# Splitting a fold on GpSimd over two slots, and re-timing what stands around it, in a fused Fourier-mixing and gated-MLP kernel

## The chip, the core and the metric

The kernel runs on one core of a Trainium2 chip, as one launch. The metric is the device time of that launch in microseconds (us), as a median over runs. Five engines work side by side and meet through semaphores: TensorE (PE in the profile; its weight loads are listed apart as PEld), VectorE (DVE), ScalarE (ACT), GpSimd (POOL) and SyncE (SP, which here only issues transfers). Each engine takes its own instructions in program order.

## The reference

The input x has 8 batches of 3008 rows of 256 values. Each batch goes through a two-dimensional Fourier transform of which the real part is kept, and every one of the 24064 rows then goes through a two-layer block with a sigmoid gate, 256 to 2048 to 256:

```python
X = np.fft.fft(x, axis=1)
X = np.fft.fft(X, axis=2)
x = X.real.astype(np.float32).reshape(24064, 256)
h = x @ w_in
g = h * (1.0 / (1.0 + np.exp(-1.702 * h)))
out = g @ w_out
```

All inputs and outputs are float32, and w_in and w_out arrive as float64 words that the kernel converts itself.

## The kernel before, in words

The transform along the rows is split as 3008 = 47 x 64 and done in two levels of small matrix products; the transform along the 256 columns is folded into w_in once (`fold_w`), so that the block works on half as many columns with real and imaginary parts (`wcs`). The output product uses a fast scheme of block matrix multiplication (seven products for eight), one level inside each step and a second level over pairs of steps: the sums and differences it needs come from `sums` and `deeper` on the activations and from `differences` and `small_weights` on w_out.

**Steps and slots.** The work is a list of 384 steps: 8 batches (b), 3 blocks each (blk), 2 halves (hh), and 8 pairs of hidden blocks (p, NP = 8). A batch is therefore 48 steps, and `t0 = 48 b` is its first. The main loop runs over slots t; a slot holds parts of several steps:

- `begin(t + 1)` and `second(t)`: the two halves of the hidden product x, each 8 matmuls of 128x64 weights (`L478`, tile x). Step t uses the PSUM bank `b0` or `b1` by the parity of t.
- `product(t - 3, 0)`, `product(t - 3, 1)`, and `small_products`: the output products into banks `o0` to `o4` (tile po, `L478` and `L623`).
- `middle`, `forward`, `activate_back` on ACT (`L542`, `L555`, `L562`).
- On DVE, in this order: `backward(t)` (`L503`, reads x from PSUM), `doubled(t + 1)` (`L548`, reads x from PSUM and has to be done before `second(t + 1)` may add to the same bank), `sums(t - 2)` (`L577`, `L578`), `deeper` (`L595`, twice a slot), and once in eight slots the steps that combine and store an output tile (`L703`, `L726`, `L745`, `L677`).
- On POOL: `sums(t - 1)` (`L574`, `L575`), two of the four sums of a step.

The first 8 steps are different: they use `hidden`, `rows` and `activate`, need one PSUM bank more each, and run while w_in and w_out are still being converted.

**The next batch.** Beside the block for batch b, the transform of batch b + 1 is prepared. `extra` holds calls by slot; they run at the end of their slot, in the order in which they were put down. `turn` and `load_x` bring x in; `fold1(b, c, nc.gpsimd)`, for c = 0 to 7, adds mirrored rows and columns of x in place on POOL (`L201`, `L203`, `L205`, `L206`, for c = 0 also `L195` to `L197`); `mix1(b, m)`, for m = 0 to 3, multiplies two folded chunks by the first-level matrices on PE (`L230`, tile ps) and copies the result back to xt on ACT (`L233`); `spill`, `fill` and `rotate` turn the layout through DRAM; `stage2` is the second level (`L332`, with the transposes `L338` on DVE).

**PSUM banks.** There are eight: b0 to b2 and o0 to o4. `bank(name)` without a tag takes the next of the list `spare`. For the first slots the list is b0, b1, b2, o4; from slot 8 on it is set at the end of every slot t to b2 and `b{t % 2}`, so that `mix1` and `stage2` in slot t take the bank in which the x of step t was, and begin(t + 2) needs it next:

```python
        if t >= NP:
            spare[:] = ["b2", f"b{t % 2}"]
```

In slot t with (t - 3) divisible by 8, from slot 11 on, a new output tile begins and `begin(t + 1)` is put ahead of `product(t - 3, 0)`.

Of the kernel before, what the change touches and what calls it, by code (L numbers as in the profile page):

```python
# [29 lines left out]
ALU = mybir.AluOpType  # L30
# [9 lines left out]
NU, NG = 2, 12  # L40
# [10 lines left out]
def free(ap, offset, *dims):  # L51
    return bass.AP(ap.tensor, ap.offset + offset, [list(ap.ap[0])] + [list(d) for d in dims])
# [59 lines left out]
def kernel(ctx: ExitStack, tc, x, w_in, w_out, tab1, tab2, out):  # L112
    nc = tc.nc
    B, S, D = x.shape
    DF = w_in.shape[1]
    H = D // 2
# [10 lines left out]
    op = ctx.enter_context(tc.tile_pool(name="op", bufs=2, space=SB))  # L127
# [21 lines left out]

        return w[rows, jj * NM:jj * NM + 64]  # L150

    spare = ["b0", "b1", "b2", "o4"]

    def bank(name, tag=None):
        if tag is None:
            tag = spare.pop(0)
            spare.append(tag)
        return psp.tile([128, 512], F32, tag=tag, name=name)
# [25 lines left out]

    e0 = {}

    def fold1(b, c, eng):

        t = xt[0:64 + NA]
        if c == 0:  # L190

            e, t0 = cv.tile([NA, 2, D], F32, tag="e", name="e"), xt[0:NA]
            e0[b] = e
            fwd, rev = free(t0, 1, [31 * D, 2], [1, H - 1]), free(t0, D - 1, [31 * D, 2], [-1, H - 1])
            eng.tensor_tensor(e[:, :, 1:H], fwd, rev, op=ALU.add)  # L195
            eng.tensor_copy(free(e[:], 0, [D, 2], [H, 2]), free(t0, 0, [31 * D, 2], [H, 2]))
            eng.tensor_tensor(e[:, :, H + 1:D], fwd, rev, op=ALU.subtract)  # L197

        at, up = 2 * c * D, (31 - 2 * c) * D
        ends = free(t, up, [-D, 2], [H, 2])  # L200
        eng.tensor_tensor(ends, ends, free(t, at, [D, 2], [H, 2]), op=ALU.add)  # L201
        low = free(t, at + 1, [D, 2], [1, D - 1])
        eng.tensor_tensor(low, low, free(t, up + D - 1, [-D, 2], [-1, D - 1]), op=ALU.add)  # L203
        fwd, rev = free(t, at + 1, [D, 2], [1, H - 1]), free(t, at + D - 1, [D, 2], [-1, H - 1])
        eng.tensor_tensor(free(t, up + 1, [-D, 2], [1, H - 1]), fwd, rev, op=ALU.add)  # L205
        eng.tensor_tensor(free(t, up + H + 1, [-D, 2], [1, H - 1]), fwd, rev, op=ALU.subtract)  # L206
# [114 lines left out]
    def stage2(b, blk):  # L321

        pq, t4 = pqp.tile([128, 2, 512], F32, tag="pq", name="pq"), t4t[b]
        pqt[b, blk] = pq
        m = m2 if b else m2f
        ps = [bank("ps2") for _ in range(NU)]
        for cs in range(2):
            for h in range(2):
                for g in range(4):
                    for u in range(NU):  # L330
                        rows, at = slice(64 * u, 64 * u + 64), cs * 256 + h * 128
                        nc.tensor.matmul(ps[u][32 * g:32 * g + 32, at:at + 128], lhsT=m[rows, cs, h * RUN:(h + 1) * RUN],  # L332
                                         rhs=t4[rows, 4 * blk:4 * blk + 4, cs * H + 32 * g:cs * H + 32 * g + 32],
                                         start=True, stop=True)
        for cs in range(2):
            for u in range(NU):

                nc.vector.transpose(free(pq[:], cs * 512 + u * RUN, [256, 2], [NU * RUN, 4], [1, RUN]),  # L338
                                    free(ps[u][:], cs * 256, [128, 2], [32, 4], [1, 32]))
# [46 lines left out]
    def low_up(key, lo=0, n=1024):  # L386

        nc.scalar.activation(pre[key][2][:, lo:lo + n].bitcast(F32), raw[key][:, lo:lo + n, 0], ACTF.Copy, scale=2.0 ** -29,
                             bias=2.0 ** 23)
# [72 lines left out]
    NP = NF // 2  # L462
# [5 lines left out]
    def width(t):  # L468

        return 226 if steps[t][1:3] == (0, 1) else 256  # L470

    def two(ap, n):
        return free(ap, 0, [256, 2], [1, n])

    def halves(out, lhs, rhs, **how):

        for c0 in (0, 64):
            nc.tensor.matmul(out[c0:c0 + 64], lhsT=lhs[:, c0:c0 + 64], rhs=rhs, skip_group_check=True, **how)  # L478

    def operands(t, cs, i):  # L480
        b, blk, hh, p = steps[t]
        f = 2 * p + i
        return wcs[cs][:, f * 128:(f + 1) * 128], pqt[b, blk][:, cs, hh * 256:hh * 256 + width(t)]

    def hidden(t):

        n = width(t)
        pa, pb = bank("pa"), bank("pb")
        for ps, cs in ((pa, 0), (pb, 1)):
            for i in range(2):  # L490
                halves(ps[:, i * 256:i * 256 + n], *operands(t, cs, i), start=True, stop=True)
        v = sp.tile([128, 512], F32, tag="v", name="v")
        nc.scalar.copy(two(v[:], n), two(pa[:], n))
        vb[t] = v, pa, pb
# [28 lines left out]
    def begin(t):  # L523

        n = width(t)
        x = xb[t] = bank("x", f"b{t % 2}")
        for i in range(2):
            halves(x[:, i * 256:i * 256 + n], *operands(t, 0, i), start=(i == 0), stop=False)
# [28 lines left out]
    def backward(t):  # L557
        reversed_sum(t, gt.pop(t), xb.pop(t), ALU.subtract)
# [237 lines left out]
    ends = n0 + 4 - 28 * NM  # L796
# [72 lines left out]
    def at(t, fn, *args):  # L869
        extra.setdefault(t, []).append((fn, args))  # L870
# [16 lines left out]
    at(4, rotate, 0, 4, NG)  # L887
    for i in range(NCK):
        at(7 + i, differences, i)
        at(9 + i, small_weights, i)  # L890
    for b in range(B):
        t0 = b * NBLK * NF
        late = 0 if b else 3
        if b + 2 < B:
            at(t0 + 10, turn, b + 2)
        if b + 1 < B:
            for c in range(NCH):
                at(t0 + 7 + 2 * c + late, fold1, b + 1, c, nc.gpsimd)
                if c % 2:
                    at(t0 + 8 + 2 * c + late, mix1, b + 1, c // 2)  # L900
            at(t0 + 24 + late, spill, b + 1)
            at(t0 + 29 + late, fill, b + 1)
            if b + 2 < B:
                at(t0 + 33 + late, load_x, b + 2)
            at(t0 + 36 + late, rotate, b + 1)
        for blk in range(NBLK):
            nxt = (b, blk + 1) if blk + 1 < NBLK else (b + 1, 0)
            if nxt[0] < B:
                at(t0 + blk * NF + 8, stage2, *nxt)
                at(t0 + blk * NF + 9, nyquist, *nxt)  # L910

    for t in range(n + LAG):
        if t < NP:
            hidden(t)
            if t == 0:
                low_up(in2)
                nyquist(0, 0)
                low_down(in2)
            if t in rows_at:
                first_row(rows_at[t])  # L920
            if t >= LAG:
                for part in range(2):
                    product(t - LAG, part)
            if t in early:
                fold_w(early[t])
            if t:
                activate(t - 1)
            rows(t)
            if t == NP - 1:
                for ahead in range(2):  # L930
                    middle(NP + ahead)
                begin(NP)
        else:
            if t < n:
                if t + 2 < n:
                    middle(t + 2)
                second(t)
            heads = [(product, t - LAG, 0)] + [(begin, t + 1)] * (t + 1 < n)
            for fn, *args in heads[::-1] if t >= NP + LAG and (t - LAG) % NP == 0 else heads:
                fn(*args)  # L940
            product(t - LAG, 1)
            small_products(t - LAG, (1, 2, 4, 7))
            small_products(t - LAG - 1, (5, 6, 3))
            if t == NP:
                activate(t - 1)
            if t < n:
                forward(t)
            if NP < t <= n:
                activate_back(t - 1)
                sums(t - 1, nc.gpsimd)  # L950
            swap(t - LAG - 2)
            if t < n:
                backward(t)
        if NP <= t + 1 < n:
            doubled(t + 1)
        if t >= NP:
            sums(t - 2, nc.vector)
            deeper(t - 2, 0)
            deeper(t - 3, 1)
        if t >= LAG:  # L960
            combine(t - LAG)
            combine_small(t - LAG - 1)
            combine_last(t - LAG - 2, 0)
            combine_last(t - LAG - 3, 1)
        if t == NP:
            held += [hp.tile(shape, F32, tag="h", name="held") for shape in
                     ([128, 2, 4, 2, 64], [128, 2, 4, 2, 64], [128, 4, 256], [128, 1024])]
        if t >= NP:
            spare[:] = ["b2", f"b{t % 2}"]
        for fn, args in extra.get(t, ()):  # L970
            fn(*args)

# [27 lines left out]
```

## Time and profile before

| What | Value |
|---|---|
| Median of 3 runs | 1928.61 us (1924.86 to 1929.21) |
| Span of the profiled execution | 1926.1 us, granted TensorE clock 0.996 |
| PE busy | 1892.3 us, 98% of the span |
| DVE busy | 1549.2 us, 80% |
| ACT busy | 875.6 us, 45% |
| POOL busy | 786.5 us, 41% |
| Transfers | 104.92 MB, mean 54 GB/s |

The first line is what is compared. The profile is of one execution with each instruction's start and end. Busy time on PE is a union of overlapping matmuls, so a wait on PE shows as idle time only where it is longer than the tail of the matmul before it; shares of the whole span are means over stages that differ. The stretch of a batch in which the next batch is folded and mixed is slots t0 + 7 to t0 + 22; in the last batch there is nothing to fold, so that the same slots there show the block alone.

### The profile page before, as it was taken

Reading aid. Unit: us, or ns where it says so; the run is one execution under the profiler, and the core shown is the slowest. Engines: PE = TensorE matmul, PEld = TensorE weight load, DVE = VectorE, ACT = ScalarE, POOL = GpSimd, SP = SyncE. Lnnn points to the kernel's source line nnn. Section 1 sums busy time; section 2 is a strip of 40 time slices with the busy share of each in tenths; the row PEclk is TensorE's granted clock in tenths of the full one; section 3 lists DMA queues with packets and bytes.
Section 4 is the critical chain, followed back from the end, with each engine's and each line's share of the span. In section 5 each row is a group of like instructions: output and inputs, shape, how many; then the busy total and the mean of one; then the engine's idle time right before and its main releaser. Section 6 shows DMA issues by size and latency. Waiting matters only on the chain.

```text
span 1926.1 us, 51018 instructions
## 1 busy us (share of the span) xinstructions
PE 1892.3 (98%) x21392; PEld 1376.7 (71%) x21392; DVE 1549.2 (80%) x3011; ACT 875.6 (45%) x1868; POOL 786.5 (41%) x1073
## 2 busy tenths in 40 slices
PE   8989999999999999999999999999999999999998
PEld 5666877767776777767777677776777767778775
DVE  7658787888788877898778977888787988878876
ACT  5634444444444444444444444444444444444442
POOL 4475223643245432463235532355223652223332
PEclk9999999999999999999999999999999999999999
DMA  8731360336212362214523164032631232202201
GB/s 279 164 50 14 81 87 18 51 49 115 24 14 49 49 120 18 35 28 72 98 18 50 22 109 56 15 58 44 101 33 23 18 48 47 29 13 18 24 16 23
DMA packets 145398, 104.92 MB, mean 54 GB/s; under 512 B 104914, under 2 KB 127986, under 8 KB 143984
## 3 DMA queue, kind: packets, MB, share of 16 engines
q1 hardware_dynamic: 143952, 101.14, 31.4%
q8 instruction: 167, 2.74, 0.6%
q10 hardware_dynamic: 1216, 0.52, 0.1%
q14 instruction: 63, 0.52, 0.1%
HBM read 58.38 MB, written 48.01 MB: 55 GB/s over the span
## 4 chain that ended last, share of the span: by engine, by line
PE 83%; DVE 11%; ACT 3%; POOL 1%; issue 1%; DMA 0%; SPq 0%; DVEq 0%; ACTq 0%; POOLq 0%
PE po L478 37%; PE x L478 29%; PE po L623 12%; DVE r L595 4%; DVE h L503 2%; DVE g L548 1%; PE ps L332 1%; PE ps L230 1%; DVE s L577 1%; DVE s L578 1%; ACT xt L233 1%; DVE held L577 1%; PE ps L283 1%; ACT g L542 1%; DVE os L677 1%
## 5 line engine op out<-in xcount | busy, mean ns | idle before, releaser
L478 PE MATMUL x<-pq,wcs 128*64 128x256 f32 (+1 forms) x6016 | 771.5, 377 | 9.0 <-DVE g L548 4.6
L555 ACT ACTIVATE h<-x 128x512 f32<-128x512 f32 (+1 forms) x376 | 221.5, 589 | 793.1 <-PE x L478 697.3
L478 PE MATMUL po<-s,wo 128*64 128x256 f32 (+1 forms) x4512 | 571.6, 375 | 3.0 <-DVE s L577 1.9
L478 PEld LDWEIGHTS x<-pq,wcs 128*64 128x64 f32 x6016 | 426.7, 137 | 180.8 <-issue 12.3
L574 POOL TENSOR_TENSOR s<-h 128x256 f32<-128x256 f32 (+1 forms) x282 | 204.6, 726 | 852.4 <-issue 614.6
L478 PEld LDWEIGHTS po<-s,wo 128*64 128x64 f32 x4512 | 334.0, 137 | 150.6 <-DVE s L577 2.3
L503 DVE TENSOR_TENSOR h<-g,x 128x512 f32<-128x512 f32 (+2 forms) x440 | 255.5, 592 | 208.7 <-ACT h L555 208.1
L542 ACT ACTIVATE g<-nb,af 128x256 f32<-128x256 f32 (+1 forms) x752 | 335.4, 496 | 2.0 <-DVE h L512 0.8
L548 DVE SCALAR_TENSOR_TENSOR g<-x,g 128x512 f32<-128x512 f32 (+1 forms) x376 | 254.4, 677 | 76.5 <-PE x L478 76.2
L478 PE MATMUL po<-h,wo 128*64 128x256 f32 (+1 forms) x1824 | 264.9, 376 | 0.7 <-DVE u L703 0.7
L562 ACT ACTIVATE h<-h 128x512 f32<-128x512 f32 (+1 forms) x376 | 231.1, 615 | 0.2 <-DVE h L503 0.2
L575 POOL TENSOR_TENSOR s<-h 128x256 f32<-128x256 f32 (+1 forms) x282 | 208.6, 740 | 0.0
L595 DVE TENSOR_TENSOR r<-h 128x256 f32<-128x256 f32 (+1 forms) x368 | 205.1, 598 | 0.0
L478 PE MATMUL po<-held,wo 128*64 128x256 f32 (+1 forms) x1504 | 194.1, 375 | 0.0
L623 PE MATMUL po<-r,held 128*64 128x128 f32 (+1 forms) x2208 | 185.6, 271 | 0.0
L478 PEld LDWEIGHTS po<-h,wo 128*64 128x64 f32 x1824 | 136.5, 137 | 59.9 <-DVE u L703 1.2
L577 DVE TENSOR_TENSOR s<-s,h 128x256 f32<-128x256 f32 (+1 forms) x282 | 167.0, 592 | 3.3 <-POOL s L574 3.3
L623 PEld LDWEIGHTS po<-r,held 128*64 128x64 f32 x2208 | 143.2, 137 | 23.2
L574 POOL TENSOR_TENSOR held<-h 128x256 f32<-128x256 f32 (+1 forms) x94 | 69.0, 734 | 212.0 <-DVE held L726 94.0
L478 PEld LDWEIGHTS po<-held,wo 128*64 128x64 f32 x1504 | 111.7, 137 | 49.3 <-DVE held L577 1.6
L578 DVE TENSOR_TENSOR s<-h,s 128x256 f32<-128x256 f32 (+1 forms) x282 | 133.3, 473 | 9.7
L623 PE MATMUL po<-h,wo 128*64 128x128 f32 (+1 forms) x1472 | 112.3, 270 | 0.0
(106 smaller groups left out, 1717.3 us busy)
## 6 DMA issues: line engine op xcount, KB each, us to landing
out_dram<-os SPq DMA_DIRECT2D x284, 64.0 KB
Td<-xt SPq DMA_DIRECT2D x14, 768.0 KB
t<-Td SPq DMA_DIRECT2D x7, 1536.0 KB
xt<-in_x_dram SPq DMA_DIRECT2D x14, 512.0 KB
xt<-Xr SPq DMA_DIRECT2D x14, 512.0 KB
nb<-pq SPq DMA_DIRECT2D x23, 256.0 KB
out_dram<-os SPq DMA_DIRECT2D x96, 56.0 KB
Xr<-in_x_dram SPq DMA_DIRECT2D x7, 752.0 KB
```

Source lines behind the costliest of these rows:

```text
L478: nc.tensor.matmul(out[c0:c0 + 64], lhsT=lhs[:, c0:c0 + 64], rhs=rhs, skip_group_check=True, **how)
L503: nc.vector.tensor_tensor(free(h[:], 512 + at + m - 1, [256, 2], [RUN, blocks], [-1, m]), *ins, op=op)
L542: nc.scalar.activation(g[:, i * 256:i * 256 + n], nbt[b, blk][:, hh * 256:hh * 256 + n], ACTF.Copy, scale=af2[:, f:f + 1])
L548: nc.vector.scalar_tensor_tensor(g, two(xb[t][:], n), 2.0, g, op0=ALU.mult, op1=ALU.add)
L555: nc.scalar.activation(two(h[:], n), two(xb[t][:], n), ACTF.Gelu_apprx_sigmoid)
L562: nc.scalar.activation(g, g, ACTF.Gelu_apprx_sigmoid)
L574: eng.tensor_tensor(s1, a21, a22, op=ALU.add)
L575: eng.tensor_tensor(s3, a11, a21, op=ALU.subtract)
L577: eng.tensor_tensor(s2, s1, a11, op=ALU.subtract)
L578: eng.tensor_tensor(s4, a12, s2, op=ALU.subtract)
L595: nc.vector.tensor_tensor(out, i0, i1, op=how)
L623: nc.tensor.matmul(sub(k)[64 * side:64 * side + 64, :w], lhsT=lhs, rhs=rhs, start=(p == 0 and k in (1, 2)), stop=(p == NP - 2), skip_group ...
```

## The change

It has six parts, all of them about when things are done; the arithmetic stays as it is.

1. `fold1` is cut in two parts: part 0 (`L201`, `L203`, and for c = 0 also the three operations on e) and part 1 (`L205`, `L206`). Part 0 goes in the slot where the whole fold went, part 1 in the next slot.
2. `mix1` therefore moves one slot back, to t0 + 11, 15, 19 and 23. For the first batch `late` grows from 3 to 4 on top: parts of folds in slots 11 to 26, mixes in 15, 19, 23 and 27. `rotate` stays where it was.
3. `small_weights` moves ahead: from slots 9 to 12 to slots 8, 8, 9, 10.
4. `spare` has six banks in the first slots (o2 and o3 are added); in slots 6 and 7 it is cut to the o banks and b2, so that b0 and b1 are free.
5. `begin(8)` moves, in slot 7, from the end of the slot to a place ahead of the output products of step 4.
6. From slot 8 on `spare` is `b{t % 2}`, b2 in place of b2, `b{t % 2}`; and `stage2` does the transposes of one bank first, then those of the other.

Part 1 of the fold is meant to spread POOL's work evenly over the slots, parts 3 to 5 to shorten the start, part 6 to free the bank that x needs next sooner.

```diff
-    spare = ["b0", "b1", "b2", "o4"]
+    spare = ["b0", "b1", "b2", "o2", "o3", "o4"]
...
-    def fold1(b, c, eng):
+    def fold1(b, c, part, eng):
...
-        eng.tensor_tensor(ends, ends, free(t, at, [D, 2], [H, 2]), op=ALU.add)
-        low = free(t, at + 1, [D, 2], [1, D - 1])
-        eng.tensor_tensor(low, low, free(t, up + D - 1, [-D, 2], [-1, D - 1]), op=ALU.add)
+        if part == 0:
+            eng.tensor_tensor(ends, ends, free(t, at, [D, 2], [H, 2]), op=ALU.add)
+            low = free(t, at + 1, [D, 2], [1, D - 1])
+            eng.tensor_tensor(low, low, free(t, up + D - 1, [-D, 2], [-1, D - 1]), op=ALU.add)
+            return
...
-        for cs in range(2):
-            for u in range(NU):
+        for u in range(NU):
+            for cs in range(2):
...
-        at(9 + i, small_weights, i)
+        at(max(7 + i, 8), small_weights, i)
...
-        late = 0 if b else 3
+        late = 0 if b else 4
...
-                at(t0 + 7 + 2 * c + late, fold1, b + 1, c, nc.gpsimd)
+                for part in range(2):
+                    at(t0 + 7 + 2 * c + part + late, fold1, b + 1, c, part, nc.gpsimd)
                 if c % 2:
-                    at(t0 + 8 + 2 * c + late, mix1, b + 1, c // 2)
+                    at(t0 + 9 + 2 * c + late, mix1, b + 1, c // 2)
...
-            at(t0 + 36 + late, rotate, b + 1)
+            at(t0 + 36 + 3 * (late > 0), rotate, b + 1)
...
+            if t == NP - 2:
+                spare[:] = [tag for tag in spare if tag[0] == "o"] + ["b2"]
             hidden(t)
+            if t == NP - 1:
+                begin(NP)
...
-                begin(NP)
...
-            spare[:] = ["b2", f"b{t % 2}"]
+            spare[:] = [f"b{t % 2}", "b2"]
```

More of the change, by code (lines that the diff above doesn't have):

```diff
@@ L185 @@
     e0 = {}
-    def fold1(b, c, eng):
+    def fold1(b, c, part, eng):
         t = xt[0:64 + NA]
-        if c == 0:
+        if c == 0 and part == 0:
             e, t0 = cv.tile([NA, 2, D], F32, tag="e", name="e"), xt[0:NA]
```

## The prediction, made before the change was run

> **What bounds the kernel now.** I read the page's first part, then the busy time by stretches, then the order of time around the places where PE stops.
>
> ```profile
> PE 1892.3 (98%) x21392; PEld 1376.7 (71%) x21392; DVE 1549.2 (80%) x3011; ACT 875.6 (45%) x1868; POOL 786.5 (41%) x1073
> ```
>
> PE sets the end, and only 33.8 us of its span are idle. The first stretch below is slots t0+11 to t0+26 of a batch with six of its eight folds in it, the second the same slots of the last batch, which folds nothing (columns: length, then busy time of PE, PEld, DVE, ACT, POOL).
>
> ```profile
> 813.57:894.20 80.63, 78.81 (x937) 56.46 (x938) 69.02 (x127) 37.31 (x84) 41.77 (x57) 1.00 0.31 56
> 1741.18:1813.21 72.03, 72.03 (x866) 60.67 (x864) 57.84 (x127) 33.42 (x76) 22.10 (x33) 1.00 0.19 19
> ```
>
> PE has four mixes more in the first: 1.46 + 3 x 1.02 = 4.5 us by the chain of waits. The rest, 80.63 - 72.03 - 4.5 = 4.1 us, is lost. Idle time shows only 1.8 of it, because each wait also costs the overlap of matmuls: one lasts 376 ns and a new one starts every 108 ns (20 in 2.16 us), so an interruption costs some 0.27 us beside the idle time. With the same number of instructions DVE is busy 11.2 us longer. Its L595 alone (the same stretches, DVE only):
>
> ```profile
> 813.57:894.20 80.63, 21.63 (x32) 1.00 0.31 56
> 1741.18:1813.21 72.03, 12.13 (x32) 1.00 0.19 19
> ```
>
> The order of time shows why:
>
> ```profile
> 827.76 1.27 POOL L203 TENSOR_TENSOR xt<-xt 111x510 f32<-111x510 f32 x1
> 827.88 1.40 DVE L577 TENSOR_TENSOR held<-held,h 128x226 f32<-128x226 f32 x1
> ...
> 829.11 0.75 POOL L205 TENSOR_TENSOR xt<-xt 111x254 f32<-111x254 f32 x1
> ...
> 829.32 0.80 DVE L578 TENSOR_TENSOR held<-h,held 128x226 f32<-128x226 f32 x1
> ...
> 829.83 0.88 POOL L206 TENSOR_TENSOR xt<-xt 111x254 f32<-111x254 f32 x1
> 830.04 2.47 DVE L595 TENSOR_TENSOR r<-h 128x226 f32<-128x226 f32 x2
> ...
> 833.06 0.64 DVE L503 TENSOR_TENSOR h<-g,x 128x448 f32<-128x448 f32 x2
> 833.63 0.61 DVE L548 SCALAR_TENSOR_TENSOR g<-x,g 128x452 f32<-128x452 f32 x1
> ...
> 833.85 1.08 PE L230 MATMUL ps<-xt,w 47*64 47x256 f32 x12 [0.59 <-DVE h L503]
> ```
>
> While POOL folds, L577 takes 1.40 us, not 0.38, and the two L595 2.47, not 0.8: one whole fold in one slot makes DVE 3.1 us late here. L503 then comes late, and the mix on PE waits for the bank it reads. In the first batch POOL itself is late:
>
> ```profile
> 118.95 0.60 PE L478 MATMUL po<-s,wo 128*64 128x226 f32 x4 [1.91 <-DVE s L577]
> 127.47 0.70 PE L230 MATMUL ps<-xt,w 47*64 47x256 f32 x3 [4.63 <-POOL xt L206]
> ```
>
> **What the skill says.** The Trainium skill, "SBUF — State Buffer", section "SBUF: two separate sides", says that a DVE operation with two SBUF inputs and a GpSimd operation that reads SBUF take turns on a shared port pair, the loser blocked for the whole instruction of the other. The trace agrees: L577 ends 0.25 us after the L203 beside it. L503 and L548, with one input in PSUM, keep their 0.65 and 0.61 us under folds. "PSUM — Partial Sum Buffer", section "PSUM bank collisions raise a hardware error", wants accesses of different engines to a bank kept apart by semaphores per bank, not per address; so a mix has to wait for L503, and the next x for the copy L233.
>
> **Part by part: splitting the folds (1) and moving the mixes (2), batches 1 to 6.** Nothing is added; eight folds of 0.36 + 1.33 + 0.77 + 0.80 = 3.3 us become halves of 1.7 and 1.6. A slot is 4.65 us of PE (37.2 for eight). DVE needs 0.69 + 0.69 + 0.42 + 0.43 + 2 x 0.40 = 3.0 us of it, plus 2.0, 1.6, 1.4 and 0.7 in the four combining slots t0+10 to 13 (and 18 to 21). A fold makes DVE 11.2 / 6 = 1.9 us longer on average: 1.0 where it met combining steps that read PSUM (slot 11), 3.1 where it didn't (13). Now a plain slot takes 3.0 + 1.1 = 4.1 us with half a fold, which fits; before, every odd slot had up to 3.0 + 3.1 = 6.1.
>
> What PE lost by slot (start of second(t) to the next, against the same slot without folds): slot 11 0.45 and slot 19 0.4, x waiting for the mix's second copy on ACT; the mix after slot 14 1.2; slot 16 0.8, x waiting for L548 (0.63 idle); six more at 0.1 to 0.17: 3.7 us.
>
> - The ACT waits (0.85) go: the mixes leave the slots ahead of 11 and 19, where begin() stands first, and the bank that x needs is now copied first (part 6): free 0.6 us sooner, and behind one more product of 0.43 us. L233 ended 0.29 us too late.
> - The 1.2 at the mix and the 0.8 at slot 16 go if DVE is at most 1.5 us behind its usual start in slots 15 and 16, 1.75 us after second(). By the sums above it is behind 1.6 us in slot 11 (from 10: 5.0 + 1.1 against 4.45), and then the half fold falls beside L703, L503 and L548, which it doesn't block; 0.4 in slot 12, 0.7 in 13, 0.6 in 14, about none from 15. L548 may end as late as 4.2 us into a slot of that width; in slot 11 the mix behind it leaves 5.7.
> - I keep 1.1 us per batch for what combining and half folds still cost in slots 10 to 13 and 18 to 21, and for the mix now waiting with its first matmul for the bank, not its fifth. Gain 2.6 x 6 = 15.6 us; ends 0.85 x 6 = 5 and 3.7 x 6 = 22.
>
> **The first batch (2, 3).** second(13) to second(15) took 134.35 - 115.70 = 18.65 us; two slots of 4.2 and a mix of 1.46 make 9.9: 8.8 lost to POOL being late. POOL works without pause from 91.1 us: four differences at 0.79, small weights at 1.8 for four, sums at 1.3, the first fold 4.9. New order: sums(10) end at 114.9 (118.65 before), while product(10) needs them near 116.5; the folds of chunks 0 and 1 end near 127, and the mix, now after slot 15, is due at about 128. I take 8.3 of the 8.8. The four later waits (at 155.29, 156.54, 169.03 and 187.61: 0.72, 0.16, 0.52, 0.32, and 4 x 0.27) are 2.8 us, of the kind above: 1.7 of them. Together 10.0; ends 5 and 11.6.
>
> **The start (4, 5).** x of step 8 waited 0.80 us for L548, which waited for begin(8) behind 3.5 us of products; now begin(8) stands ahead of them, DVE comes to L548 at 90.6, not 91.1, and 0.5 to 1.0 us goes. pb waited 1.38 us for a bank at 45.72, pa 0.34 at 62.06, pb 0.24 at 85.44: six banks take these away, but ACT and DVE, preparing weights, are busy 30 and 32 of 50 us there, so that PE may wait for them instead. I take 2.0 in all; ends 0.5 and 4.
>
> **The rest (6).** The four transposes of stage2 free the first bank 0.7 us sooner; only slot 24 of the first batch (0.32 at 187.61) waited for that, counted above. The later spill has five slots or more to fill(); no engine waits for it in the list of waits, and rotate() comes 6 slots (28 us) after fill in the first batch, 7 before: nothing.
>
> Sum: 15.6 + 10.0 + 2.0 = 27.6; 1928.6 - 27.6 = **1901.0 us**.
>
> **Rivals.**
>
> - The blocking only moves: DVE still pays 1.9 us a fold, the halves add up in the combining slots, and x waits for L548 there. For it: slots 10 to 13 need 17.9 of 18.6 us without a fold, and four halves fall on them, as two folds did. Against: in slot 11 a fold cost DVE 1.0, not 3.1. Then 5.1 (ACT waits) + 8.3 + 1 = 14 us: 1914.
> - Slower: mixes now stand in odd slots and their first matmul waits for L503 of the same slot. If DVE is late in all of them as it was at 832.60, 24 mixes lose 1.2 us: +28.8 - 12.0 (first batch and start) = +16.8: 1945. Against: L503 starts 1.75 us into a slot, the mix at 4.65.
> - No change: POOL's chain of 91 to 128 us holds the first batch as before and the halves win nothing: 1927. Against: the order of POOL above brings sums(10) 3.7 us forward.
>
> **How the numbers follow.** Forecast 0.68, first rival 0.20, slower 0.08, no change 0.04. Faster 0.88, same 0.04, slower 0.08. If all loss goes, 22 + 11.6 + 4 = 37.6, the time is 1891; the first rival with little won at the start gives 1916. Range 1890 to 1916.
>
> **What would show it.** Right: L595 as long in sum as before or a little shorter, but the DVE waits of x and mix gone from the list of PE's waits; a batch of 229.4 us, not 231.96; the 4.63 and 1.91 us waits gone. The first rival: x waiting for L548 in slots 12 to 14 and 20 to 22. The slower one: L230 waiting for L503 at every mix. I am wrong in the first batch if POOL's sums still come after the product that wants them.

## The result, and the profile after

The changed kernel takes 1907.08 us, the median of four runs (1906.63 to 1908.82); the kernel before, run on the same chip, 1928.67 us (1924.86 to 1929.21). The ratio is 0.9894, with a 95% interval of 0.9877 to 0.9911. Faster, and within the range of 1890 to 1916, but 6 us above the forecast of 1901.0. In the profiled executions the span fell from 1926.1 to 1905.5 us. The lines named from here on stand one or two further down than before: `L478` is now `L480`, `L503` `L505`, `L548` `L550`, `L595` `L597`, `L703` `L705`; the fold is `L202` and `L204` (part 0), `L207` and `L208` (part 1).

The first part of the page after:

```profile
PE 1881.4 (99%) x21392; PEld 1360.9 (71%) x21392; DVE 1540.6 (81%) x3011; ACT 877.5 (46%) x1868; POOL 789.9 (41%) x1073
```

PE still sets the end and still has 24.1 us idle (33.8 before). What it waited for tells more. The head of PE's list of waits before (who waited for whom: us in total, times, longest):

```profile
PE ps L230 <- POOL xt L206: 4.6, 1, 4.6
PE x L478 <- DVE g L548: 4.6, 7, 0.8
PE ps L230 <- DVE h L503: 4.1, 7, 0.6
PE x L478 <- ACT xt L233: 3.0, 12, 0.3
...
PE po L478 <- DVE s L577: 1.9, 1, 1.9
```

and after (the line left out, in both lists, is a wait of 2.6 us in the preparation at the start):

```profile
PE x L480 <- DVE g L550: 3.7, 8, 0.5
PE po L480 <- DVE c L705: 3.5, 14, 0.4
...
PE po L480 <- issue: 2.1, 1, 2.1
PE po L480 <- DVE u L705: 1.4, 7, 0.2
```

Four of the five lines of before are gone: the mix (ps) waits neither for POOL nor for DVE, x no longer waits for the copy on ACT, and the product no longer for the sums. One is still there: x waits for `L550`. And two that were small have grown: the output products (po) wait for `L705`, the step that combines an output tile out of the banks o0 to o4, 21 times and 4.9 us in sum, where they waited twice and 0.9 us before. The line "issue" is a stop for which the profile names no cause; the first batch has it and its part below comes back to it. The same stretch as in the prediction, slots t0+11 to t0+26 of batch 3 with six folds and four mixes in them (before's begins with the mix at the end of slot 10, so that it holds four too; length, then busy time of PE, PEld, DVE, ACT, POOL), and then `L597` alone there (DVE only):

```profile
797.89:877.61 79.72, 78.46 (x940) 56.84 (x938) 67.09 (x130) 37.56 (x84) 43.04 (x58) 1.00 0.31 57
```

```profile
797.89:877.61 79.72, 18.29 (x34) 1.00 0.31 57
```

80.63 us became 79.72, and `L597` is still far from the 12.13 us that it takes where nothing is folded. A whole batch, from the x at slot 43 of batch 3 to the same x of batch 4, before and after:

```profile
970.30:1202.27 231.97, 230.07 (x2666) 166.25 (x2664) 192.09 (x376) 105.39 (x232) 96.17 (x132) 1.00 0.33 52
```

```profile
953.71:1184.34 230.63, 229.39 (x2666) 166.90 (x2664) 189.73 (x376) 105.61 (x232) 96.56 (x132) 1.00 0.33 52
```

A batch gained 1.34 us, not 2.6. Cutting the span at places that both traces have (the first pa of the start, second(8), the x of 16 matmuls at slot 43 of the first and of the last full batch) shows where 20.6 us went:

| Stretch | Before, us | After, us | Gain, us | Forecast, us |
|---|---|---|---|---|
| To the first pa | 40.32 | 39.89 | 0.4 | 0 |
| First pa to second(8) | 51.47 | 46.52 | 5.0 | 2.0 |
| second(8) to slot 43, first batch | 182.06 | 174.96 | 7.1 | 10.0 |
| Seven batches to slot 43 of the last (six with folds and mixes) | 1613.75 | 1605.62 | 8.1 | 15.6 |

### The profile page after: what moved, and what is told of

Same layout as the page of the kernel before. It is cut to its first block, busy times and chain, and to the rows that moved or that the text cites. A ratio compares the mean times of both kernels' runs of the same rounds, so it can differ in the third digit from the quotient of the medians.

```text
span 1905.5 us, 51020 instructions
## 1 busy us (share of the span) xinstructions
PE 1881.4 (99%) x21392; PEld 1360.9 (71%) x21392; DVE 1540.6 (81%) x3011; ACT 877.5 (46%) x1868; POOL 789.9 (41%) x1073
## 4 chain that ended last, share of the span: by engine, by line
PE 88%; DVE 8%; ACT 1%; DMA 1%; issue 1%; POOL 0%; SPq 0%; DVEq 0%; ACTq 0%; POOLq 0%
PE po L480 39%; PE x L480 31%; PE po L625 13%; DVE r L597 2%; PE ps L334 1%; PE ps L232 1%; DVE g L550 1%; DVE s L580 1%; DVE s L579 1%; DVE h L505 1%; DVE c L705 1%; PE ps L285 1%; DVE u L705 1%; DMA wo<-in_tab_dram 0%; PE psw L450 0%
## 5 line engine op out<-in xcount | busy, mean ns | idle before, releaser
L480 PE MATMUL x<-pq,wcs 128*64 128x256 f32 (+1 forms) x6016 | 766.2, 376 | 3.9 <-DVE g L550 3.7
L480 PE MATMUL po<-s,wo 128*64 128x256 f32 (+1 forms) x4512 | 573.0, 375 | 5.6 <-DVE c L705 3.5
L480 PEld LDWEIGHTS x<-pq,wcs 128*64 128x64 f32 x6016 | 423.3, 137 | 172.8 <-issue 11.6
L480 PEld LDWEIGHTS po<-s,wo 128*64 128x64 f32 x4512 | 330.2, 137 | 159.1 <-POOL s L576 9.2
L505 DVE TENSOR_TENSOR h<-g,x 128x512 f32<-128x512 f32 (+2 forms) x440 | 255.9, 593 | 209.5 <-ACT h L557 207.8
L550 DVE SCALAR_TENSOR_TENSOR g<-x,g 128x512 f32<-128x512 f32 (+1 forms) x376 | 254.9, 678 | 74.8 <-PE x L480 74.3
L480 PE MATMUL po<-h,wo 128*64 128x256 f32 (+1 forms) x1824 | 264.2, 376 | 1.6 <-DVE u L705 1.4
L480 PE MATMUL po<-held,wo 128*64 128x256 f32 (+1 forms) x1504 | 193.4, 375 | 0.1
L480 PEld LDWEIGHTS po<-h,wo 128*64 128x64 f32 x1824 | 132.9, 137 | 66.6 <-DVE u L705 7.6
L579 DVE TENSOR_TENSOR s<-s,h 128x256 f32<-128x256 f32 (+1 forms) x282 | 177.5, 629 | 0.1
L597 DVE TENSOR_TENSOR r<-h 128x256 f32<-128x256 f32 (+1 forms) x368 | 162.8, 484 | 0.0
L580 DVE TENSOR_TENSOR s<-h,s 128x256 f32<-128x256 f32 (+1 forms) x282 | 147.5, 523 | 9.7
L480 PEld LDWEIGHTS po<-held,wo 128*64 128x64 f32 x1504 | 110.8, 137 | 49.7 <-DVE held L579 0.5
```

The source lines that it names most:

```text
L505: nc.vector.tensor_tensor(free(h[:], 512 + at + m - 1, [256, 2], [RUN, blocks], [-1, m]), *ins, op=op)
L550: nc.vector.scalar_tensor_tensor(g, two(xb[t][:], n), 2.0, g, op0=ALU.mult, op1=ALU.add)
L579: eng.tensor_tensor(s2, s1, a11, op=ALU.subtract)
L580: eng.tensor_tensor(s4, a12, s2, op=ALU.subtract)
L597: nc.vector.tensor_tensor(out, i0, i1, op=how)
```

## The experiments

All twelve kernels are the changed kernel with one edit (e11_both: with two). Cuts of code are marked with `...`. Each was timed against the kernel before, whose median was 1927.1 to 1929.1 us beside them. "Batch" is the length of the stretch above, from slot 43 of batch 3 to slot 43 of batch 4; "Folds" tells how they are done in it.

| Run | Median, us | Ratio (95%) | Folds | Batch, us |
|---|---|---|---|---|
| changed kernel | 1907.08 | 0.9894 (0.9877 to 0.9911) | halves | 230.63 |
| e1_whole | 1908.99 | 0.9896 (0.9881 to 0.9910) | whole | 230.91 |
| e2_spare | 1913.49 | 0.9920 (0.9903 to 0.9936) | halves | 231.96 |
| e5_skip | 1905.68 | 0.9882 (0.9867 to 0.9897) | halves | 230.29 |
| e6_free | 1898.16 | 0.9841 (0.9827 to 0.9856) | halves, plain slots | 228.61 |
| e12_freewhole | 1897.05 | 0.9844 (0.9829 to 0.9859) | whole, plain slots | 228.62 |
| e9_free1 | 1899.06 | 0.9851 (0.9837 to 0.9866) | as e6_free, batch 1 too | 228.61 |
| e13_all | 1896.70 | 0.9842 (0.9825 to 0.9858) | as e12_freewhole, batch 1 too | 228.61 |
| e3_start | 1911.49 | 0.9915 (0.9899 to 0.9931) | halves | 230.61 |
| e4_small | 1906.72 | 0.9891 (0.9876 to 0.9906) | halves | 230.61 |
| e10_late | 1908.83 | 0.9904 (0.9887 to 0.9920) | halves | 230.77 |
| e11_both | 1910.46 | 0.9915 (0.9898 to 0.9931) | halves | 230.63 |
| e8_load | 1907.55 | 0.9898 (0.9881 to 0.9916) | halves | 230.62 |

### Is it the split? (e1_whole)

Both halves of a fold in the first of their two slots; mixes, banks and all else as changed.

```diff
-                    at(t0 + 7 + 2 * c + part + late, fold1, b + 1, c, part, nc.gpsimd)
+                    at(t0 + 7 + 2 * c + late, fold1, b + 1, c, part, nc.gpsimd)
```

> The changed kernel with each fold whole again in its odd slot; mixes, banks and start stay as changed. In the changed kernel a batch (1 to 6) takes 230.65 us, before 231.96. If splitting the folds is what gave the 1.3 us, a batch goes back to 231.5 or more and the time to 1912 or more. If moving the mixes and turning the bank order gave it, a batch stays at 230.6 to 230.8 and only the first batch may lose a little: 1907 to 1909.

The batch takes 230.91 us with whole folds: of 1.34 us the split brings 0.28. The moved mixes and the new bank order keep 1.06 together. The order of time on PE shows what the whole fold costs now; x of batch 4 waits for the `L550` of slot 14:

```profile
1050.49 0.98 PE L480 MATMUL x<-pq,wcs 128*64 128x226 f32 x8 [1.62 <-DVE g L550]
```

and what the halves cost in the changed kernel (slot 11, the end of slot 13, and slot 19 of the same batch):

```profile
1031.63 1.37 PE L480 MATMUL po<-s,wo 128*64 128x226 f32 x12 [0.35 <-DVE c L705]
1043.97 0.98 PE L480 MATMUL x<-pq,wcs 128*64 128x226 f32 x8 [0.50 <-DVE g L550]
1068.65 0.65 PE L480 MATMUL po<-h,wo 128*64 128x256 f32 x4 [0.20 <-DVE u L705]
1069.90 1.52 PE L480 MATMUL po<-s,wo 128*64 128x256 f32 x12 [0.16 <-DVE c L705]
```

Two stops, the one of 1.62 us and one of 0.16 in slot 19, have turned into four of 1.21 us in sum. A stop costs more than its idle time: that of 0.50 us makes its slot 0.67 us wider than the same slot of e6_free below, where nobody waits (from the start of second(t) to the next). The split trades one wait for others.

How a half does it is in the order of time of slots 10 and 11 in batch 2 of the changed kernel:

```profile
566.18 0.87 POOL L207 TENSOR_TENSOR xt<-xt 111x254 f32<-111x254 f32 x1
...
566.51 0.80 DVE L580 TENSOR_TENSOR s<-h,s 128x226 f32<-128x226 f32 x1
...
567.02 0.87 POOL L208 TENSOR_TENSOR xt<-xt 111x254 f32<-111x254 f32 x1
...
567.23 0.94 DVE L597 TENSOR_TENSOR r<-r,h 128x256 f32<-128x256 f32 x1
567.26 1.73 PE L480 MATMUL x<-pq,wcs 128*64 128x226 f32 x16
...
568.20 0.42 DVE L597 TENSOR_TENSOR r<-h,r 128x256 f32<-128x256 f32 x1
...
568.54 0.94 DVE L705 TENSOR_TENSOR u<-u,po 128x256 f32<-128x256 f32 x2
...
569.01 0.20 PEld L480 LDWEIGHTS po<-h,wo 128*64 128x64 f32 x4 [0.43 <-DVE u L705]
```

Part 1 of the fold stands at the end of slot 10. Beside it `L580` takes 0.80 us, not 0.40, and the first `L597` 0.94, not the 0.41 that it takes in e6_free's slot 10, where no fold stands. `L705` then begins 1.28 us after the x at 567.26. It has to empty the banks of the old output tile before the new tile's first products, which begin in just this slot, may use them.

The wait for `L550` at the end of slot 13 comes from the half in slot 12, here in batch 4:

```profile
1039.71 0.91 DVE L597 TENSOR_TENSOR r<-r,h 128x226 f32<-128x226 f32 x1
...
1040.66 0.80 DVE L597 TENSOR_TENSOR r<-h,r 128x226 f32<-128x226 f32 x1
...
1042.73 0.65 DVE L505 TENSOR_TENSOR h<-g,x 128x448 f32<-128x448 f32 x2
```

Beside the half `L580` and the two `L597` take 0.74, 0.91 and 0.80 us; without a fold, in the same place of e6_free, they take 1.3 us less in sum. `L505` starts 3.44 us into slot 13 (second(13) began at 1039.29), against 2.21 in e6_free, and `L550` comes after it.

### No half ahead of a new output tile (e5_skip, e6_free)

e5_skip moves only the halves that fall in slots 10 and 18, a slot later each.

```diff
-                    at(t0 + 7 + 2 * c + part + late, fold1, b + 1, c, part, nc.gpsimd)
+                    to = t0 + 7 + 2 * c + part + late
+                    at(to + (b > 0 and to % 8 == 2), fold1, b + 1, c, part, nc.gpsimd)
```

> The changed kernel, but in batches 1 to 7 the half fold of slots 10 and 18 is put off to slots 11 and 19. Theory: half folds in slots 10 and 18 make L705 late, and the first output products of a new tile wait for its banks (14 waits on c, 7 on u in the list of waits): those of batches 1 to 6 go, slots 11 and 19 fall from 5.04 and 5.37 us to 4.4 and 4.7, a batch takes 229.3 to 230.0, unless slots 12 and 13 then lose the same for L550. Rival: the loss in slots 11 and 19 comes from the moved mixes or from ACT: no change there, 230.65.

All three waits for `L705` are gone from the batch, and this one is left, at the end of slot 13:

```profile
1046.24 0.98 PE L480 MATMUL x<-pq,wcs 128*64 128x226 f32 x8 [1.15 <-DVE g L550]
```

So the half in slots 10 and 18 was what made the products wait. Slots 11 and 19 fall by 0.73 and 0.50 us. But the two halves that now meet in slots 11 and 19 make `L550` late by more: slots 13, 21 and 22 grow by 0.89 in sum. That leaves 230.29 us, a gain of 0.34, short of the 229.3 to 230.0 expected. The delay moves on to the next thing that DVE has to deliver.

e6_free, for batches 2 to 6, puts all halves into "plain" slots, in which DVE combines nothing (in 5, 13 and 21 it still finishes and stores a tile), starting two slots ahead of the batch, and no fold in slots t0+10 to 12 and 18 to 20; the mixes go to slots 3, 9, 16 and 23.

```diff
+    FREE = -2, -1, 0, 1, 5, 6, 7, 8, 9, 13, 14, 15, 16, 17, 21, 22
...
-                    at(t0 + 7 + 2 * c + part + late, fold1, b + 1, c, part, nc.gpsimd)
+                    to = 7 + 2 * c + part + late if b < 2 else FREE[2 * c + part]
+                    at(t0 + to, fold1, b + 1, c, part, nc.gpsimd)
...
-                    at(t0 + 9 + 2 * c + late, mix1, b + 1, c // 2)
+                    at(t0 + (9 + 2 * c + late if b < 2 else (3, 9, 16, 23)[c // 2]), mix1, b + 1, c // 2)
```

> The changed kernel, but from batch 2 on no half fold stands in slots 10 to 12 and 18 to 20, where tiles are combined; the folds begin two slots before the batch and take slots -2 to 1, 5 to 9, 13 to 17, 21, 22, with mixes after 3, 9, 16 and 23. Theory: what is left of the loss (about 2.8 us of 230.65 a batch) comes from half folds beside combining steps, so a batch of 2 to 6 falls to 228 to 229 us and the time to 1895 to 1900. Rival: half folds cost DVE the same wherever they stand and PE loses it in other slots: a batch stays within 0.5 of 230.65.

It beats both kernels: 1898.16 us. The batch, then `L597` alone in it:

```profile
949.31:1177.92 228.61, 228.39 (x2667) 168.30 (x2664) 191.56 (x376) 105.34 (x232) 97.94 (x132) 1.00 0.33 53
```

```profile
949.31:1177.92 228.61, 50.46 (x97) 1.00 0.33 53
```

and the same for `L597` in the changed kernel:

```profile
953.71:1184.34 230.63, 45.97 (x97) 1.00 0.33 52
```

DVE is blocked longer in the faster kernel: `L597` takes 50.46 us against 45.97, and DVE as a whole is busy for 191.56 against 189.73. PE nevertheless stops once in the batch, for 0.22 us. The time that POOL takes from DVE isn't what PE pays for; what counts is which operation of DVE stands behind it.

The mixes moved too, and no run moved them alone. Slot by slot they don't explain the gain: a mix adds 1.1 us to its slot in 9 or 16 as it did in 15. With the two mixes of slots 11 and 19 counted at what they cost in their new slots, these slots still gain 1.3 us, about what e5_skip had shown to hang on `L705`, and slot 13 gains 0.7, the wait for `L550`.

### Whole folds in the plain slots (e12_freewhole, e9_free1, e13_all)

If so, the split shouldn't matter once the folds stand right. e12_freewhole is e6_free with both halves in the first of their two slots:

```diff
-                    to = 7 + 2 * c + part + late if b < 2 else FREE[2 * c + part]
+                    to = 7 + 2 * c + part + late if b < 2 else FREE[2 * c]
```

> The same plain slots for batches 2 to 6, but each fold whole again in the first of its two slots. If only where DVE is blocked counts, and not how long at a time, this is as fast as halves in plain slots: 228.6 us a batch and 1898 us. If the split matters once placement is right, a whole fold (up to 3 us of DVE) makes x or the mix wait in the slot after it, 0.3 to 0.8 us in each of eight: 230 to 233 us a batch and 1905 to 1920 us.

```profile
951.52:1180.14 228.62, 228.40 (x2667) 168.28 (x2664) 189.85 (x376) 105.35 (x232) 97.92 (x132) 1.00 0.34 53
```

228.62 against 228.61 us, and the same single stop. In plain slots a split fold and a whole one cost PE the same. The rival's 0.3 to 0.8 us in eight slots did not come. Nor did its 3 us of DVE: what DVE's operations beside a fold take above their usual time sums to 0.8 to 1.7 us a fold here. The one of slot 5, which ends in slot 6:

```profile
1003.84 2.36 DVE L597 TENSOR_TENSOR r<-h 128x256 f32<-128x256 f32 x2
...
1006.75 0.64 DVE L505 TENSOR_TENSOR h<-g,x 128x512 f32<-128x512 f32 x1
...
1010.45 0.69 DVE L505 TENSOR_TENSOR h<-g,x 128x512 f32<-128x512 f32 x1 [0.73 <-ACT h L557]
```

`L505` starts 2.77 us into slot 6, 1.0 later than in the same slot without a fold beside it; in slot 7 DVE waits for ACT again and is on time.

e9_free1 gives batch 1 plain slots too, in e6_free's manner but from slot 5 on, with its last mix in slot 27, and for that its transfers four slots later:

```diff
-        late = 0 if b else 4
+        late = 0 if b > 1 else 4
...
+    FIRST = 5, 6, 7, 8, 9, 13, 14, 15, 16, 17, 21, 22, 23, 24, 25, 26
...
```

> Like the kernel with half folds in plain slots only, with batch 1 arranged so too (before, only batches 2 to 6 were). My theory (a half fold costs PE only where it falls on a slot in which a new output tile begins): batch 1 falls by the 2.05 us that the other batches fell by, 1896 us against 1898.2. The rival (the 2 us came from folds begun ahead of the batch, in slots t0 - 2 to t0 + 1, which batch 1 does not do here): batch 1 keeps its 230.6 us and the time stays at 1898.

No gain: batch 1 takes 230.93 us (230.74 in e6_free). Its waits have fallen from 1.20 us of idle time to 0.46, but a new stop stands near its end, with no releaser in the profile, and the transfer engines are full around it, for some 20 us (the last column but one of the second fence is their busy share):

```profile
487.43 0.65 PE L480 MATMUL x<-pq,wcs 128*64 128x256 f32 x4 [1.36 <-issue]
```

```profile
480.00:485.00 5.00, 5.00 (x104) 3.52 (x90) 3.62 (x9) 1.91 (x4) 1.42 (x2) 1.00 1.04 196
485.00:490.00 5.00, 3.64 (x40) 2.40 (x38) 1.91 (x5) 1.38 (x3) 0.49 (x1) 1.00 1.06 110
```

Without the 1.36 us and a tail of 0.27, the prediction's estimate, batch 1 would be 229.3, so the early slots are not all of it; but the run didn't show that by itself. e13_all tried it without moving the transfers: whole folds in e12_freewhole's slots for batches 1 to 6, batch 1 beginning two slots early as well.

```diff
-                    to = 7 + 2 * c + part + late if b < 2 else FREE[2 * c]
+                    to = 7 + 2 * c + part + late if b < 1 else FREE[2 * c]
...
-                    at(t0 + (9 + 2 * c + late if b < 2 else (3, 9, 16, 23)[c // 2]), mix1, b + 1, c // 2)
+                    at(t0 + (9 + 2 * c + late if b < 1 else (3, 9, 16, 23)[c // 2]), mix1, b + 1, c // 2)
```

> Whole folds in the plain slots for batches 1 to 6, begun two slots ahead of the batch in batch 1 too, its load and layout turn at the changed kernel's slots. If the gain in the earlier run for batch 1 was eaten by PE's stop without a releaser beside 20 us of full transfer engines (those were put later there), batch 1 now has at most 0.95 of transfer share, no such stop, and falls from 230.7 to about 228.7 us: 1895 to 1896 us. If batch 1 can't gain, because the load for its folds lands too late in batch 0 or for another reason, it keeps 230.7 us or grows, and the time is 1897 us or more.

Batch 1 takes 489.92 - 261.20 = 228.72 us, without such a stop, as expected. The time lies between the two that were expected, 1895 to 1896 us and 1897 or more. At 1896.70 us (1895.27 to 1898.00) it is the lowest of the study, but not told apart from e12_freewhole's (1896.72 to 1898.99).

### The bank order (e2_spare)

The old order of the two spare banks, with the transposes of `stage2` still one bank after the other:

```diff
-            spare[:] = [f"b{t % 2}", "b2"]
+            spare[:] = ["b2", f"b{t % 2}"]
```

> The changed kernel with the old order of the two spare banks (b2 first, then that of x). My prediction counted on this order and the moved mixes together for 0.85 us a batch. If the order matters, x after a mix waits for the second copy on ACT again, some 0.3 to 0.6 us at each of 28 mixes: 1915 to 1922. If the moved mixes alone took the wait away (a product of 0.43 us stands between), the time stays within 2 us of 1907.

The batch is 1.33 us longer (on the mean of batches 1 to 6 it is 1.1), and the time of 1913.49 us lies between the two expected ranges. The head of PE's list of waits, in which the second line was 0.2 us, once, in the changed kernel:

```profile
PE x L480 <- DVE g L550: 5.0, 8, 1.2
PE x L480 <- DVE pq L340: 4.0, 7, 0.9
```

The transposes now empty the bank that the next x needs last: slot 9, behind `stage2`, is 0.67 us wider. The other half of the 1.33 is the wait for `L550` at the end of slot 13, 1.15 us in place of 0.50; why the order lengthens it, this run doesn't show. No wait for the mix's copy on ACT comes back: moving the mixes was enough to end those. So the bank order has to go with the order of the transposes; what the pair is worth against the old pair was not tried.

### The start (e3_start)

Four spare banks and begin(8) at the end of slot 7, as before.

```diff
-    spare = ["b0", "b1", "b2", "o2", "o3", "o4"]
+    spare = ["b0", "b1", "b2", "o4"]
...
-            if t == NP - 2:
-                spare[:] = [tag for tag in spare if tag[0] == "o"] + ["b2"]
...
-            if t == NP - 1:
-                begin(NP)
...
+                begin(NP)
```

> The changed kernel with the old start: four banks in rotation and begin(8) at the end of slot 7. I had put both at 2.0 us (0.5 to 4). In the one profile of each, second(8) starts at 91.79 us before and at 86.41 in the changed kernel, but four kernels with the same start have it at 85.5 to 89.4. If the new start gives what these say, the time is 3 to 5 us above 1907 and second(8) starts at 90 or later, with waits of pb, pa and x for DVE of 1.6, 0.3 and 0.8 us again. If ACT and DVE set the pace there, less than 2 us and second(8) inside 85.5 to 89.4.

First pa to second(8) takes 50.45 us against 46.52: these two parts are worth 3.9 us, and the time says 4.4 (1911.49 against 1907.08). second(8) itself starts at 89.31 us, within the range of the other expectation, but only because the first pa came early here, at 38.86 against 39.89. PE's longest stops there:

```profile
44.26 1.08 PE L480 MATMUL pb<-pq,wcs 128*64 128x256 f32 x8 [1.39 <-DVE h L505]
...
59.58 1.08 PE L480 MATMUL pa<-pq,wcs 128*64 128x256 f32 x8 [1.91 <-DVE h L505]
...
89.31 0.98 PE L480 MATMUL x<-pq,wcs 128*64 128x226 f32 x8 [0.80 <-DVE g L550]
```

With six banks, 0.27 us at the last pb and the following are left of these:

```profile
86.41 0.98 PE L480 MATMUL x<-pq,wcs 128*64 128x226 f32 x8 [0.44 <-DVE g L550]
```

### The first batch (e4_small, e10_late, e11_both, e8_load)

Small weights at their old slots; the first batch's folds a slot earlier, and with them its mixes, spill, fill and load of x, all of which `late` had moved; both together:

```diff
-        at(max(7 + i, 8), small_weights, i)
+        at(9 + i, small_weights, i)
```

> The changed kernel with small_weights in slots 9 to 12 again. I had put the first batch's gain down to POOL's order: small weights ahead, folds a slot later. If the small weights matter, POOL gives sums(10) late again, PE waits 1 to 2 us for it near 115 us and the time is 2 to 6 us above 1907. If the later folds and mixes alone did it, no wait of PE over 0.5 us between 105 and 140 us and a time within 1.5 us of 1907.

```diff
-        late = 0 if b else 4
+        late = 0 if b else 3
```

> The changed kernel with late at 3 again for the first batch: its half folds in slots 10 to 25, mixes in 14, 18, 22, 26. If the later slot is needed for POOL, the first mix or the sums wait for POOL 1 to 4 us near 120 us and the time rises by as much. If the small weights and the split are enough, no such wait, and the time is within 1.5 us of 1907; even slots may cost the mixes ahead of slots 19 and 27 some 0.3 us each for ACT.

> The changed kernel with the small weights at their old slots and the first batch's folds and mixes one slot earlier again, both at once; each alone left the first batch as it was. If one of the two is needed (either will do), the waits of 1.9 and 4.6 us for sums and mix on POOL return at about slots 13 to 15, the stretch from second(8) to slot 43 is 180 to 182 us, not 175, and the time is 1912 to 1914 us. If something else shortened the first batch (bank order, halves), the stretch stays at 175 us and the time at 1907.

second(8) to slot 43 takes 174.7 us in each of the first two, against 174.96, and 177.5 with both undone. But these lengths contain a stop of varying length. It stands in slot 41 of the first batch in every trace of the study, 0.66 to 2.13 us long, and no releaser is named for it. In the changed kernel:

```profile
255.64 0.43 PE L480 MATMUL po<-s,wo 128*64 128x256 f32 x1 [2.10 <-issue]
```

Without its idle time the stretch is:

| Run | Stretch, us | Stop in slot 41, us | Without it, us |
|---|---|---|---|
| before | 182.06 | 0.66 | 181.4 |
| changed kernel | 174.96 | 2.10 | 172.9 |
| e4_small | 174.66 | 1.91 | 172.8 |
| e10_late | 174.68 | 0.81 | 173.9 |
| e11_both | 177.49 | 0.90 | 176.6 |

Undoing the small weights alone changes nothing. Undoing the later slot alone costs 1.0 us: in e10_late the product waits for the sums again, as its expectation had it, and the first mix stops with no releaser named.

```profile
114.29 0.60 PE L480 MATMUL po<-s,wo 128*64 128x226 f32 x4 [2.27 <-DVE s L579]
123.31 0.29 PE L232 MATMUL ps<-e,w 47*64 47x129 f32 x1 [1.01 <-issue]
```

With both undone the waits for the sums and for POOL return, smaller than before:

```profile
111.27 0.60 PE L480 MATMUL po<-s,wo 128*64 128x226 f32 x4 [0.48 <-DVE s L579]
116.14 0.60 PE L480 MATMUL po<-held,wo 128*64 128x226 f32 x4 [0.64 <-DVE held L579]
122.43 0.70 PE L232 MATMUL ps<-xt,w 47*64 47x256 f32 x3 [2.20 <-POOL xt L208]
```

The times agree: 1906.72, 1908.83 and 1910.46 us, against 1907.08. So the small weights and the later slot carry 3.7 us of the 8.5 that the first batch gained without the stop, less than the 5 to 7 us that e11_both was expected to give back. The other 4.8 belong to what stays in e11_both (the mixes a slot after their second fold, halves, banks and the transposes' order); which of these was not taken apart.

The stop in slot 41 is 1.4 us longer than before's (0.66 at 268.12), which is why the stretch gained 7.1 us, not 8.5. e8_load meant to separate it from the load of x, which is put down in slot 37:

```diff
-                at(t0 + 33 + late, load_x, b + 2)
+                at(t0 + 33 + 2 * late, load_x, b + 2)
```

> The changed kernel with the first batch's load_x in slot 41 in place of 37. PE stands 2.1 us at 255.6 in the changed kernel, 0.7 at 268.1 before, with no releaser in the trace, while all transfer engines are busy with load_x. If the load is the cause[...], the stop vanishes or moves with the load, and 0 to 2 us are won. If it belongs to that place in PE's program, it stays at the same instruction with about 2 us.

The stop was still there, 1.28 us at 254.25. But the edit did not move the load. Its first transfer in the changed kernel and in e8_load:

```profile
236.91 0.41 SPq L182 DMA_DIRECT2D xt<-in_x_dram  x1
236.35 0.41 SPq L182 DMA_DIRECT2D xt<-in_x_dram  x1
```

Measured back from the x at slot 43, less the stop, that is the same moment in both. So the run says nothing on the cause.

## Why the prediction was right, and where it was off

- **Faster, by about 1%.** Right. PE was the bound and stayed it; the waits of 4.63 and 1.91 us and those of the mix for `L503` are gone, as "What would show it" had it, and so are those of x for ACT. Those of x for DVE, which it counted on too, only fell from 4.6 to 3.7 us, and the batch of 229.4 us was not reached.
- **Parts 1 and 2, batches 1 to 6: 15.6 us forecast, 8.1 measured.** This is the step that failed: "I keep 1.1 us per batch for what combining and half folds still cost in slots 10 to 13 and 18 to 21". Per batch 3.7 us were counted as lost and 1.3 came back, so 2.4 us stayed, not 1.1. e6_free recovers 2.0 of them, so the count of what could be won was about right (231.97 - 228.61 = 3.36). The step looked at `L548`'s deadline only, and mis-sized that. It found DVE 1.6 us behind in slot 11, which is what came (`L505` starts 3.39 us into the slot, not 1.75), and took it as harmless because the fold "falls beside L703, L503 and L548, which it doesn't block". True, but `L703` itself begins late behind a blocked `L595`, and the first products of the new tile wait for it in that very slot: 1.2 us in slots 11 and 19. For slot 13 it had DVE 0.7 us behind; it was 1.7, and the slot is only 4.0 us wide without waits, not the mean of 4.65: another 0.7 us.
- **The reason for the split.** A half was taken to fit a slot and a whole not (4.1 against up to 6.1 us of 4.65). The 3.1 us in the second sum were read from the fold of slot 13. In batch 4 of the kernel before, summed as above, that one and the next cost DVE 3.2 and 3.4 us, the other six 1.3 to 1.8 (that of slot 11, put at 1.0, 1.4); in plain slots e12_freewhole measures 0.8 to 1.7, which about fits. Why a fold costs twice as much in some places was not tested. The split is worth 0.28 us a batch where the change put it, and nothing in plain slots. The 0.8 at slot 16 went with whole folds too (e1_whole), that is, without it, and so did the mix's wait of 1.2; there x now waits for `L550` in its place.
- **The first rival** (1914 us, the blocking only moves) is half right: x does wait for `L550`, at the end of slot 13, for 0.50 us, and the waits for `L705` are of its kind. The time lies midway between it and the forecast.
- **The other two rivals** were wrong: no mix waits for `L505` in the list after, and POOL's chain held the first batch no longer.
- **First batch: 10.0 us forecast, 7.1 measured.** The waits for POOL went as worked out. 1.4 us were given back in the stop at slot 41, which no step had. The prediction ascribed 8.3 us to POOL's new order; undoing the two edits that change it most gives back only 3.7.
- **The start: 2.0 us forecast, 5.0 measured.** Mis-sized: the list of waits before showed 1.38, 0.34, 0.24 and 0.80 us, 2.8 in sum, and the prediction discounted these for busy ACT and DVE. That was the term: e3_start shows that the banks and the place of begin(8) are worth 3.9 of the 5.0, more than those waits' idle time. Where the other 1.1 come from was not tried. That this stretch and the first batch together gained 12.1 us, with 12.0 forecast, is luck: two errors of 3 us cancel.
- **The blocking itself.** That the loser of the port is blocked for a whole instruction (the Trainium skill, "SBUF — State Buffer", section "SBUF: two separate sides") agrees with the trace after: `L597` takes 0.94 us beside `L208`, not 0.41, and ends 0.28 us after it. What the blocking costs PE depends on what stands behind it, as the runs show.

## What to carry to other kernels

When one engine slows another that has slack, list everything that the slowed engine has to deliver and by when, in each slot, before cutting the disturbing work smaller. Moving it away from the slots with a tight delivery was worth 2.3 us a batch here as a whole (e1_whole to e12_freewhole) and 2.0 in halves, halving it in place 0.3. An engine's busy or blocked time may grow while the kernel gets faster.

## What the runs showed of the hardware that was not expected

- PE stops for 0.7 to 2.1 us with nothing in the profile that it waits for. All fourteen traces have such a stop in slot 41 of the first batch, after some 15 us of transfer engines at about 1.0 of their time; batch 1 has one only in e9_free1, after some 15 us of the same. Full transfer engines alone don't cause it, though: around the load of x in batches 1 to 5 they are as full for some 20 us in the changed kernel, and PE runs on. One 5 us piece of that, in batch 3:

```profile
905.00:910.00 5.00, 5.00 (x60) 3.70 (x58) 3.39 (x8) 1.91 (x4) 1.42 (x2) 1.00 1.08 125
```

Some runs have a further stop in batch 3 (0.68 us at 868.24 in e13_all, 2.16 at 871.78 in e9_free1), after 10 us at 1.0 and 0.86; e6_free, at 1.01 and 0.88 from 860 to 870 us, has none. The cause stays open.
- The start up to the first pa moved by 4 us (39.05 to 42.87 us) between twelve kernels that begin alike, while the stretch from there to second(8) repeated within 0.13 us (46.45 to 46.58). Differences of a few us between single profiles are read from marks, not from spans.
